# Attention with top-k and a routed mixture of experts on one core: a constant in the fill columns, logits of a batch in two parts, a check of the logits in four parts

## Chip, cores and metric

The kernel runs on one core of a Trainium2 chip. The metric is device time in microseconds (us) of one execution, median of several runs. Engines: PE is TensorE (PEld its weight loads), DVE is VectorE, ACT is ScalarE, POOL is GpSimd, SP is SyncE, which here issues DMAs.

## What is computed

The reference, cut to what matters: attention over 8 batches, 8 heads, 576 positions and 64 features, keeping in each row only scores that reach the 32nd largest, then a mixture of 8 experts in which tokens are assigned greedily by the size of their gate logits.

```
scores = scale * np.matmul(q, k.transpose(0, 1, 3, 2))
kth = np.partition(scores, -top_k, axis=-1)[..., -top_k:-top_k + 1]
scores = np.where(scores >= kth, scores, -1e9)
attn = softmax(scores)
x = (attn @ v).transpose(0, 2, 1, 3).reshape(4608, 512)
logits = x @ w_gate
...
out[mask] = np.maximum(x[mask] @ w1[e], 0.0) @ w2[e]
```

## The kernel before, in words

**Work.** `attention` works through 32 pairs of heads, four pairs (hp 0 to 3) to a batch. A pair has nine tiles of 128 query rows by 576 keys (tile 4 holds the last 64 rows of both heads), so 288 tiles in all. After it `redo` would repeat the attention of pairs that a flag marks (none is marked here; the branch passes over it), and `moe` runs the experts.

**One tile** (`tile_ops`). PE writes the scores into one of three PSUM buffers `s` (`scores`, L218). DVE takes the eight largest of each of six chunks of 96 columns (`chunk`, L221), and from these 48 the first 24 in order (`rank`, L224 to L228). `minus` (L229) makes a bias of the 24th. ACT takes the sign of every score against it and counts with the accumulator (`sign`, L233, into `acc`). By that count, `fill` on DVE (L238) writes eight extra columns 576 to 583 of `s`: a column gets the 24th value, read per row from `st`, where its number in `tab` is under the count, and 0 elsewhere. PE moves the 24 largest out of the way with a matmul (`move` with `off`, L236), DVE takes the next eight over 584 columns (`next8`, L239), of which the last is the cut, PE moves the row back (`move` with `back`), and ACT writes the mask `r` (`relu`, L242) and so sets the buffer `s` free.

**After the tiles** of a pair, `soft` builds transposed scores with the mask in one of two PSUM buffers `pt`, ACT takes the exponential, POOL splits it into two halves of 16 bits, `values` multiplies with v, and ACT scales the result into `xb` (512 rows of the batch) and `xr` (the last 64 rows, the corner).

**Logits** (`logits`, called behind hp 3 only). Five pieces for a batch: four of 128 rows and the corner. For a piece PE transposes the 512 features (L396, four of 128 columns; two in the corner), ACT copies them to `xT` (L398), PE multiplies with the gate weights into another `pt` buffer (L402, L404), and ACT puts the eight logits into `L` (L407, L408).

**Verdict** (`verdict`, L420 to L443). On DVE, behind everything else of attention in its queue: eight instructions on the counts and cuts, three on `L` (is every logit finite, L430 to L432), a matmul on PE that sums over the rows, and a few small ones that write `flags`. All engines read the flag before `moe` starts.

**What sets the order.** `Plan` is a list scheduler: `at` gives every step an engine, a planned duration `d`, and a due time made of the period `PER` and an offset in the table `O`; among the steps that can start within a window `WIN` of the earliest, the one due first goes. The order it finds is the order of each engine's queue; the queues then run in that order and wait on semaphores. SP's queue holds the loads, the transposing DMAs (`turn`, L186, of K and Q; `q2`, L267) and the stores.

Of the kernel before, what the change touches and what calls it, by code (L numbers as in the profile page):

```python
# [99 lines left out]
def attention(tc, q,k,v,w_gate,x_out,L,flags, pairs):  # L100
# [3 lines left out]
    with ExitStack() as ctx:  # L104
# [100 lines left out]
        def tile_ops(P,i):  # L205
# [32 lines left out]
            def fill(): V.tensor_scalar(D["s"][:,576:584],tab,acc[:,col],P["st"][:,i,23:24],op0=ALU.is_lt,op1=ALU.mult)  # L238
# [149 lines left out]
        def logits(P):  # L388
            b=P["b"]; n=P["n"]; t0=(n*9+8)*PER+O["lg"]
            fin=[]  # L390
            for c in range(5):
                p=P["done"]
                D={}; w=512 if c<4 else 256
                def turn(c=c,D=D):
                    D["pt"]=ps_t.tile([128,512],F32,tag="pt",name="ptl")
                    for f in range(4 if c<4 else 2): T.transpose(D["pt"][:,f*128:(f+1)*128],P["x"][0][:,c,f*128:(f+1)*128] if c<4 else P["x"][1][:,2*f:2*f+2,:].rearrange("p a d -> p (a d)"),identf)  # L396
                def copy(D=D,w=w):
                    D["xT"]=wk.tile([128,512],F32,tag="xT",name="xT",bufs=2); A.activation(D["xT"][:,:w],D["pt"][:,:w],AF.Copy)  # L398
                def dot(c=c,D=D):
                    lg=D["lg"]=ps_t.tile([128,512],F32,tag="pt",name="lg"); xT=D["xT"]; o=(b%2)*64  # L400
                    if c<4:
                        for f in range(4): T.matmul(lg[:,:8],xT[:,f*128:(f+1)*128],wg[:,f,:],start=(f==0),stop=(f==3))  # L402
                    else:
                        for i_,(g,a) in enumerate(((0,0),(0,1),(1,0),(1,1))): T.matmul(lg[o:o+64,:8],xT[:,g*128+a*64:g*128+a*64+64],wgr[:,g,a,:],start=(i_==0),stop=(i_==3))  # L404
                def put(c=c,D=D):
                    o=(b%2)*64
                    if c<4: A.activation(L[:,b*4+c,:],D["lg"][:,:8],AF.Copy)  # L407
                    else: A.activation(L[o:o+64,32+b//2,:],D["lg"][o:o+64,:8],AF.Copy)  # L408
                t=t0+O["lgd"]*c
                p=at(t,turn,[p],take="pt",e="P",d=.436); tp=p  # L410
                p=at(t+O["l1"],copy,[p],free=[tp],take="xT",e="A",d=.48); tx=p
                p=at(t+O["l2"],dot,[p],take="pt",free=[tx],e="P",d=.9); tp=p
                p=at(t+O["l3"],put,[p],free=[tp],e="A",d=.07); fin.append(p)
            P["fin"]=at(t0,lambda: None,fin)
            P["done"]=p
        def verdict():

            n9=len(pairs)*9; npr=len(pairs)
            c=cp.tile([128,n9],F32,name="vc"); r=cp.tile([128,n9],F32,name="vr"); ok=cp.tile([128,n9],F32,name="vok")
# [4 lines left out]
            V.scalar_tensor_tensor(ok,c,8.0,ok,op0=ALU.is_le,op1=ALU.mult)
            V.scalar_tensor_tensor(ok,c,0.0,ok,op0=ALU.is_ge,op1=ALU.mult)
            V.scalar_tensor_tensor(ok,cuts,0.0,ok,op0=ALU.is_gt,op1=ALU.mult)
            good=cp.tile([128,npr+1],F32,name="good")
            V.tensor_reduce(good[:,:npr],ok.rearrange("p (n i) -> p n i",i=9),axis=AX.X,op=ALU.add)
            Lf=L.rearrange("p t e -> p (t e)"); fin=cp.tile([128,Lf.shape[1]],F32,name="fin")
# [15 lines left out]
        Ps={}; batch={}
        for n in range(len(pairs)):
# [15 lines left out]
            if P["hp"]==3 or n==len(pairs)-1:  # L462
                logits(P); batch[b]=at((n*9+8)*PER+O["lg"]+O["lgd"]*5,lambda P=P: store(P),[P["fin"]],e="D",d=2.0,late=4.0)
# [485 lines left out]
```

## Time and profile before

| | |
|---|---|
| median of 3 runs | 1474.12 us (1472.0 to 1474.5) |
| profiled execution, its own time | 1470.44 us |
| its span, first to last instruction | 1468.4 us |
| busy over the span | PE 1295.9 us (88%), DVE 1220.3 (83%), ACT 864.6 (59%), POOL 877.2 (60%) |
| attention, first score to last cut | 22.29 to 941.6 us |
| end of attention to the experts' first instruction | 941.6 to 972.03 us |
| experts | 972 to 1468 us |

The profile's page gives a busy share of the whole span, and the stages have different limits; views by stretch and by wait tell which engine ends last in a stage. A busy time counts an instruction up to the end of its write, and the next one on the engine often starts before that: what an instruction takes of its engine's queue is the distance between two starts.

### The profile page before, as it was taken

How to read it: one execution, taken by the hardware profiler on the slowest of the kernel's cores; microseconds unless marked ns; L12 is line 12 of the kernel's file. 1: busy time of each engine (PE TensorE's matmuls, PEld its weight loads, DVE VectorE, ACT ScalarE, POOL GpSimd, SP SyncE). 2: the span in 40 equal slices, each digit the busy share in tenths (PEclk: the TensorE clock that was granted, in tenths of full speed). 3: DMA queues.
4: the chain of work that ended last, by engine and by line, in shares of the span. 5: the costliest groups of instructions: out<-in, count | busy, mean ns of one | idle time of the engine just before them, and what ended most of it. 6: DMA issues, size and time to landing. Idle time of an engine off the chain costs nothing. (4 is left out here: it accounts for less than half of the span.)

```text
span 1468.4 us, 41338 instructions
## 1 busy us (share of the span) xinstructions
PE 1295.9 (88%) x14885; PEld 913.2 (62%) x14886; DVE 1220.3 (83%) x5951; ACT 864.6 (59%) x1922; POOL 877.2 (60%) x1285
## 2 busy tenths in 40 slices
PE   2888998999999999999999899832999999998997
PEld 1666776776776776677677677621655655664663
DVE  4899999999999999999999999658889878887610
ACT  2677777777777777777777787612334424324421
POOL 5688789788788788789879878502043123122211
PEclk9899999999999999999999999955999999999899
DMA  6343363354455445443543452016346346348500
GB/s 130 74 88 78 80 127 84 75 120 91 82 110 97 89 108 84 94 109 77 97 110 83 92 107 46 10 35 170 122 99 198 137 91 198 140 96 271 112 33 33
DMA packets 298149, 149.62 MB, mean 102 GB/s; under 512 B 255440, under 2 KB 280016, under 8 KB 296912
## 3 DMA queue, kind: packets, MB, share of 16 engines
q1 hardware_dynamic: 292048, 128.02, 38.5%
q0 software_dynamic: 5888, 18.88, 4.5%
q8 instruction: 119, 1.95, 0.6%
q14 instruction: 94, 0.77, 0.2%
HBM read 71.34 MB, written 18.87 MB: 61 GB/s over the span
## 5 line engine op out<-in xcount | busy, mean ns | idle before, releaser
L221 DVE MAX8 cd<-s 128x8 f32<-128x96 f32 x1728 | 383.2, 251 | 35.4 <-PE s L218 28.6
L296 POOL TENSOR_TENSOR elm<-F,ehm 128x512 f16<-128x512 f32 x256 | 294.3, 1156 | 6.3
L242 ACT ACTIVATE r<-s,st 128x576 bf16<-128x576 f32 x288 | 213.0, 740 | 98.8 <-PE s L236 93.8
L233 ACT ACTIVATE w<-s,st 128x576 uint16<-128x576 f32 x288 | 213.1, 740 | 95.0 <-DVE st L229 92.9
L895 POOL DMA_INDIRECT out_dram<-ob,idx x40 | 59.0, 1476 | 326.1 <-ACT ob L890 268.2
L239 DVE MAX8 st<-s 128x8 f32<-128x584 f32 x288 | 220.5, 766 | 10.4 <-PE s L236 6.7
L218 PE MATMUL s<-K,Q 128*128 128x512 f16 (+3 forms) x1280 | 195.3, 293 | 28.6 <-DMA Q<-nq 22.3
L856 PE MATMUL ph<-xT,w1h 128*128 128x288 f16 x1024 | 195.8, 289 | 2.0 <-DMA xT<-xs 2.0
L293 POOL TENSOR_SCALAR ehm<-F 128x512 f16<-128x512 f32 x256 | 156.0, 617 | 52.7 <-ACT F L290 52.3
L286 PE MATMUL pt<-Q,K 66*128 66x128 f16 (+1 forms) x1280 | 182.6, 217 | 0.2 <-DMA Q<-nq 0.2
L285 PE MATMUL pt<-Q,K 128*128 128x128 f16 (+1 forms) x1280 | 181.6, 216 | 0.0
L218 PEld LDWEIGHTS <-Q 128*128 128x128 f16 (+1 forms) x1280 | 105.9, 103 | 111.9 <-DMA Q<-nq 22.0
L236 PE MATMUL s<-w,off 128*128 128x512 f16 x576 | 134.1, 290 | 46.8 <-DVE s L238 26.9
L290 ACT ACTIVATE F<-pt 128x512 f32<-128x512 f32 x256 | 150.4, 596 | 20.8 <-PE pt L286 18.5
L856 PE MATMUL ph<-xT,w1l 128*128 128x288 f16 x512 | 147.6, 288 | 0.0
L364 PE MATMUL pv<-vt,E 128*64 128x65 f32 (+1 forms) x1024 | 146.4, 257 | 0.0
L236 PE MATMUL s<-w,back 128*128 128x512 f16 x576 | 120.9, 292 | 23.5 <-DVE st L239 21.7
L865 ACT ACTIVATE hh<-ph 128x288 f16<-128x288 f32 x128 | 52.4, 410 | 146.3 <-PE ph L856 145.4
L285 PEld LDWEIGHTS <-K 128*128 128x128 f16 x1280 | 118.3, 99 | 22.5 <-issue 8.7
L364 PEld LDWEIGHTS <-ehm 128*128 128x128 f16 x2048 | 116.2, 102 | 10.0 <-issue 0.5
L364 PEld LDWEIGHTS pv<-vt,E 128*64 128x64 f32 (+1 forms) x1024 | 113.0, 164 | 14.5 <-issue 3.5
L364 PE MATMUL pv<-vh,ehm 128*128 128x65 f16 x1024 | 120.8, 195 | 0.6 <-ACT F L290 0.6
(252 smaller groups left out, 3271.0 us busy)
## 6 DMA issues: line engine op xcount, KB each, us to landing
wr<-in_moe_w_dram SPq DMA_DIRECT2D x32, 1024.0 KB, 8.2
kn<-in_k_dram SPq DMA_DIRECT2D x64, 128.0 KB, 2.6
qn<-in_q_dram SPq DMA_DIRECT2D x64, 128.0 KB, 2.3
vn<-in_v_dram SPq DMA_DIRECT2D x64, 128.0 KB, 2.3
x<-xb SPq DMA_DIRECT2D x8, 1024.0 KB, 4.8
Q<-nq SPq DMA_TRANSPOSE x160, 3.3
kn<-in_k_dram SPq DMA_DIRECT2D x64, 16.0 KB, 2.3
qn<-in_q_dram SPq DMA_DIRECT2D x64, 16.0 KB, 2.2
```

The costliest lines, as they stand in the source:

```text
L218: T.matmul(s_ps[rows,a:b_],P[Q][:,qc],P[K][:,h*576+a:h*576+b_],start=(Q=="Q1"),stop=(Q=="Q2"))
L221: V.max(D["cd"][:,c*8:c*8+8],D["s"][:,576*c//NCH:576*(c+1)//NCH])
L233: A.activation(D["w"],D["s"][:,:576],AF.Sign,bias=P["st"][:,i,32:33],scale=(1+2.0**-21),accum_out=acc[:,col])
L236: T.matmul(D["s"][:,a:b_],by,w[:,a:b_],start=False,stop=True,skip_group_check=True)
L239: def next8(): V.max(P["st"][:,i,24:32],D["s"][:,:584])
L242: A.activation(r,D["s"][:,:576],AF.Relu,bias=P["st"][:,i,31:32],scale=-1.0)
L285: T.matmul(o,K2[:,kb:kb+128],Q1[:,qc],start=False,stop=False,skip_group_check=True)
L286: T.matmul(o,K3[0:66,kb:kb+128],Q2[0:66,qc],start=False,stop=(c==3 and h==sub[-1][0]),skip_group_check=True)
L293: G.tensor_scalar(D["eh"],D["E"],1.0,0.0,op0=ALU.mult,op1=ALU.add)
L296: G.tensor_tensor(el,D["E"],D["eh"],op=ALU.subtract); P["e"][i]=(D["eh"],el)
L364: for m_ in (range(N-1) if part==0 else (N-1,)): T.matmul(out,seq[m_][0],seq[m_][1],start=(m_==0),stop=(m_==N-1))
L856: P.matmul(B["ph"][:,:288],a[:,c,fs],xT[:,b+c,cs],start=(i==0),stop=(i==11))
```

## The change

It does four things. `fill` takes the constant 2^40 in place of the per-row value. The logits of a batch come in two parts: part 0 behind hp 2, with the first 384 features of the four main pieces and the first half of the corner; part 1 behind hp 3, with the last 128 features of all four pieces in one, and the second half of the corner. The puts into `L` move from ACT to DVE: copies in part 0, additions in part 1. The verdict's look at `L` comes in four parts of it. And the planner's table, period, windows and the planned durations of `fill` and `next8` have new numbers. The experts' code and the order of their instructions are the same. Line numbers behind `fill` grow by 1, behind `verdict` by 13.

```diff
-        PER=4.6166; SP=1.3822; VP=3; WPB=14; EHB=14
-        WIN={'V': 0.027, 'A': 0.079, 'G': 0.008, 'P': 0.138, 'D': 1.472}
+        PER=4.9146; SP=1.9733; VP=3; WPB=14; EHB=14
+        WIN={'V': 0.021, 'A': 0.06, 'G': 0.042, 'P': 0.137, 'D': 1.95}
...
-            def fill(): V.tensor_scalar(D["s"][:,576:584],tab,acc[:,col],P["st"][:,i,23:24],op0=ALU.is_lt,op1=ALU.mult)
+            def fill(): V.tensor_scalar(D["s"][:,576:584],tab,acc[:,col],2.0**40,op0=ALU.is_lt,op1=ALU.mult)
...
-            f_=at(t0+O["j8"],fill,[p],e="V",d=0.075)
+            f_=at(t0+O["j8"],fill,[p],e="V",d=0.12)
...
-            p=at(t0+O["y8"],next8,[p],e="V",d=0.735)
+            p=at(t0+O["y8"],next8,[p],e="V",d=0.685)
...
-        def logits(P):
+        def logits(P,part):
...
+            def piece(k,turns,w,dots,put):
+                D={}; t=t0+O["lgd"]*k
+                def turn():
+                    pt=D["pt"]=ps_t.tile([128,512],F32,tag="pt",name="ptl")
+                    for j,src in enumerate(turns): T.transpose(pt[:,j*128:j*128+128],src(),identf)
...
+                fin.append(at(t+O["l3"],lambda: put(D["lg"]),[p],free=[tp],e="V",d=.08))
...
+            if part==0:
+                for c in range(4):
+                    def dots(lg,xT):
+                        for f in range(3): T.matmul(lg[:,:8],xT[:,f*128:f*128+128],wg[:,f,:],start=(f==0),stop=(f==2))
+                    piece(c,[lambda f=f,c=c: P["x"][0][:,c,f*128:f*128+128] for f in range(3)],384,dots,lambda lg,c=c: V.tensor_copy(L[:,b*4+c,:],lg[:,:8]))
+                piece(4,*corner(0),lambda lg: V.tensor_copy(last,lg[o:o+64,:8]))
+            else:
+                def dots(lg,xT):
+                    for c in range(4): T.matmul(lg[:,c*8:c*8+8],xT[:,c*128:c*128+128],wg[:,3,:],start=True,stop=True)
+                piece(0,[lambda c=c: P["x"][0][:,c,384:512] for c in range(4)],512,dots,lambda lg: V.tensor_tensor(main.rearrange("p c e -> p (c e)"),lg[:,:32],main.rearrange("p c e -> p (c e)"),op=ALU.add))
+                piece(1,*corner(1),lambda lg: V.tensor_tensor(last,lg[o:o+64,:8],last,op=ALU.add))
...
-            V.tensor_tensor(fin,Lf,Lf,op=ALU.subtract)
-            V.tensor_scalar(fin,fin,0.0,None,op0=ALU.is_equal)
-            V.tensor_reduce(good[:,npr:],fin,axis=AX.X,op=ALU.add)
+            for k,(u0,u1) in enumerate(((0,28),(32,35),(28,32),(35,36))):
+                Lf=L[:,u0:u1,:].rearrange("p t e -> p (t e)"); w=8*(u1-u0); fin=cp.tile([128,w],F32,name=f"fin{k}")
+                V.tensor_tensor(fin,Lf,Lf,op=ALU.subtract)
+                V.tensor_scalar(fin,fin,0.0,None,op0=ALU.is_equal)
+                V.tensor_reduce(good[:,npr+k:npr+k+1],fin,axis=AX.X,op=ALU.add); whole.append(128.0*w)
...
-            if P["hp"]==3 or n==len(pairs)-1:
-                logits(P); batch[b]=at((n*9+8)*PER+O["lg"]+O["lgd"]*5,lambda P=P: store(P),[P["fin"]],e="D",d=2.0,late=4.0)
+            if P["hp"]==2: logits(P,0)
+            if P["hp"]==3:
+                P["done"]=at(P["done"]["t"]+.001,lambda: None,[P["done"],Ps[n-1]["fin"]])
+                logits(P,1); P["done"]=P["fin"]; batch[b]=at((n*9+8)*PER+O["lg"]+O["lgd"]*5,lambda P=P: store(P),[P["fin"]],e="D",d=2.0,late=4.0)
```

How the queues change shows at three places.

The queue of SP at the start (nq0 is what the transposes of the first pair's Q read, Q_226 and Q_239 or Q1_234 the two results, kn the second pair's loads of k). Before:

```order
L186 DMA_TRANSPOSE Q2_226<-nq0_159 128x9x128 [waits DMAHW3_49,Pool_49]
L158 DMA kn_231<-in_k_dram 128x256 [waits DMAHW4_49]
L159 DMA kn_231<-in_k_dram 64x64 [waits DMAHW5_49]
L158 DMA kn_231<-in_k_dram 128x256 [waits DMAHW6_49]
L159 DMA kn_231<-in_k_dram 64x64 [waits DMAHW7_49]
L186 DMA_TRANSPOSE Q1_239<-nq0_159 128x9x128 [waits DMAHW0_49,Pool_49]
L158 DMA qn_243<-in_q_dram 128x256 [waits DMAHW1_49]
```

Now:

```order
L186 DMA_TRANSPOSE Q2_226<-nq0_159 128x9x128 [waits DMAHW3_49,Pool_49]
L186 DMA_TRANSPOSE Q1_234<-nq0_159 128x9x128 [waits DMAHW4_49,Pool_49]
L158 DMA kn_236<-in_k_dram 128x256 [waits DMAHW5_49]
L159 DMA kn_236<-in_k_dram 64x64 [waits DMAHW6_49]
L158 DMA kn_236<-in_k_dram 128x256 [waits DMAHW7_49]
L159 DMA kn_236<-in_k_dram 64x64 [waits DMAHW0_49]
L158 DMA qn_264<-in_q_dram 128x256 [waits DMAHW1_49]
```

The second transpose of the first pair's Q now stands ahead of the second pair's four loads of k; before it stood behind them.

The queue of DVE in the fourth pair (tile 33), where the first put of part 0 stands in the changed kernel (lg is a piece's result in PSUM). Before:

```order
L225 MATCH_REPLACE cd2_2513<-st_1138,cd_2456 128x48 [waits DVE_49]
L221 MAX cd_2504<-s_2488 128x8
L226 MAX st_1138<-cd2_2513 128x8 [waits DVE_49]
L221 MAX cd_2504<-s_2488 128x8
L227 MATCH_REPLACE cd2_2513<-st_1138,cd2_2513 128x48 [waits DVE_49]
L221 MAX cd_2504<-s_2488 128x8
L228 MAX st_1138<-cd2_2513 128x8 [waits DVE_49]
```

Now:

```order
L226 MAX st_1138<-cd2_2506 128x8 [waits DVE_49]
L221 MAX cd_2497<-s_2478 128x8
L227 MATCH_REPLACE cd2_2506<-st_1138,cd2_2506 128x48 [waits DVE_49]
L221 MAX cd_2497<-s_2478 128x8
L228 MAX st_1138<-cd2_2506 128x8 [waits DVE_49]
L416 COPY L_61<-lg_2508 128x8 [waits PE_49]
L221 MAX cd_2497<-s_2478 128x8
L229 SCALAR_TENSOR_TENSOR st_1138<-s_2444,st_1138 128x1 [waits DVE_49]
L224 MAX st_1138<-cd_2497 128x8 [waits DVE_49]
L221 MAX cd_2537<-s_2521 128x8 [waits PE_49]
```

Between the ranks and the chunks of two tiles there is now a copy that waits for PE. The rows of the tiles around it keep their pattern; in the whole attention a rank or bias (L224 to L229) follows right behind the instruction whose result it reads 546 times before and 540 times now.

The end of attention in DVE's queue (rs belongs to `values` of the last pair, vc, vr and vok to the verdict on the counts). Before:

```order
L378 RECIPROCAL rs_21710<-rs_21710 128x4 [waits DVE_49]
L344 TENSOR_SCALAR rs_21723<-pv_21705 128x1 [waits PE_49]
L378 RECIPROCAL rs_21723<-rs_21723 128x1 [waits DVE_49]
L420 TENSOR_SCALAR vc_21793<-acc_158 128x288
L421 TENSOR_SCALAR vr_21794<-vc_21793 128x288 [waits DVE_49]
L422 TENSOR_SCALAR vr_21794<-vr_21794 128x288 [waits DVE_49]
L423 TENSOR_TENSOR vok_21795<-vr_21794,vc_21793 128x288 [waits DVE_49]
L424 SCALAR_TENSOR_TENSOR vok_21795<-vc_21793,vok_21795 128x288 [waits DVE_49]
L425 SCALAR_TENSOR_TENSOR vok_21795<-vc_21793,vok_21795 128x288 [waits DVE_49]
L426 SCALAR_TENSOR_TENSOR vok_21795<-cuts_157,vok_21795 128x288 [waits DVE_49,Pool_49]
L428 TENSOR_REDUCE good_21803<-vok_21795 128x32 [waits DVE_49]
L430 TENSOR_TENSOR fin_21805<-L_61 128x288 [waits Activation_49]
```

Now:

```order
L416 COPY L_61<-lg_21818 128x8 [waits PE_49]
L345 TENSOR_SCALAR rs_21844<-pv_21828 128x1 [waits PE_49]
L379 RECIPROCAL rs_21844<-rs_21844 128x1 [waits DVE_49]
L417 COPY L_61<-lg_21841 64x8 [waits PE_49]
L421 TENSOR_TENSOR L_61<-lg_21860,L_61 128x32 [waits PE_49]
L422 TENSOR_TENSOR L_61<-lg_21865,L_61 64x8 [waits DVE_49,PE_49]
L428 TENSOR_SCALAR vc_21873<-acc_158 128x288
L429 TENSOR_SCALAR vr_21874<-vc_21873 128x288 [waits DVE_49]
L430 TENSOR_SCALAR vr_21874<-vr_21874 128x288 [waits DVE_49]
```

The last puts stood in ACT's queue and so beside the verdict's instructions on the counts; now they stand on DVE ahead of these.

## Rows read from the trace of the kernel before

**Rows 1.** Busy us by stretch: length; PE, PEld, DVE, ACT, POOL (count); clock, DMA, GB/s.

```profile
55.40:941.30 885.90, 819.17 (x11127) 619.31 (x11124) 828.91 (x4644) 677.05 (x1587) 735.40 (x1137) 0.99 0.44 90
```

**Rows 2.** Waits of DVE in 56 to 941 us: us in total, times, longest.

```profile
DVE cd L221 <- PE s L218: 10.5, 31, 1.2
DVE st L239 <- PE s L236: 5.7, 15, 1.0
DVE s L238 <- PE s L236: 3.4, 14, 0.3
DVE s L238 <- ACT w L233: 2.1, 14, 0.2
```

**Rows 3.** Timeline of DVE inside attention: start us, duration us, instruction.

```profile
506.53 0.19 DVE L224 MAX8 st<-cd 128x8 f32<-128x48 f32 x1
506.64 0.27 DVE L238 TENSOR_SCALAR s<-tab,acc,st 128x8 f32<-128x8 f32 x1
506.82 0.08 DVE L225 MATCH_VALUE_LOAD cd<-st,cd 128x8 f32 x1
...
507.12 0.21 DVE L226 MAX8 st<-cd 128x8 f32<-128x48 f32 x1
507.36 0.09 DVE L227 MATCH_VALUE_LOAD cd<-st,cd 128x8 f32 x1
```

**Rows 4.** Timeline of DVE in the experts, an instruction with one per-row operand.

```profile
1002.45 0.22 DVE L735 TENSOR_SCALAR w8c<-rev,win 128x8 f32<-128x8 f32 x1
1002.58 0.17 DVE L742 TENSOR_SCALAR pi<-pos 128x36 int32<-128x36 f32 x1
```

**Rows 5.** Timeline of DVE in the experts, a small read of PSUM.

```profile
979.52 0.18 DVE L677 TENSOR_TENSOR cm<-pc,dm 128x32 f32<-128x32 f32 x1
979.63 0.24 DVE L695 TENSOR_SCALAR base<-iTs,lo 128x32 f32<-128x32 f32 x1
```

**Rows 6.** Timeline of SP's queue at the start.

```profile
15.27 1.32 SPq L186 DMA_TRANSPOSE Q<-nq  x1
16.64 0.59 SPq L158 DMA_DIRECT2D kn<-in_k_dram  x1
...
19.00 1.33 SPq L186 DMA_TRANSPOSE Q<-nq  x1
```

**Rows 7.** Timeline of POOL at the start: the last step of the first pair's Q.

```profile
13.30 1.27 POOL L181 TENSOR_TENSOR nq<-sc,nq 128x576 f16<-128x576 f32 x1
```

**Rows 8.** Timeline of PE at the start: its first matmul.

```profile
22.29 3.06 PE L218 MATMUL s<-K,Q 128*128 128x512 f16 x12 [22.29 <-DMA Q<-nq]
```

**Rows 9.** Busy by stretch: a pair with logits, then the three pairs behind it, twice.

```profile
368.20:398.10 29.90, 28.43 (x354) 22.30 (x354) 26.79 (x153) 22.17 (x53) 21.28 (x35) 0.94 0.49 98
398.10:482.50 84.40, 78.59 (x1093) 58.64 (x1090) 80.16 (x450) 65.64 (x154) 74.51 (x114) 1.00 0.49 94
...
597.00:627.90 30.90, 29.45 (x358) 22.43 (x357) 27.44 (x154) 22.20 (x53) 20.36 (x33) 0.93 0.45 93
627.90:713.30 85.40, 78.85 (x1090) 59.14 (x1087) 80.09 (x448) 65.72 (x154) 75.44 (x116) 0.98 0.46 94
```

**Rows 10.** Timeline of ACT at the end of attention.

```profile
954.48 0.32 ACT L346 ACTIVATE xr<-pv,rs 128x64 f32<-128x64 f32 x1 [0.19 <-DVE rs L378]
...
957.68 0.18 ACT L407 ACTIVATE L<-lg 128x8 f32<-128x8 f32 x1 [0.72 <-PE lg L402]
...
963.93 0.17 ACT L408 ACTIVATE L<-lg 64x8 f32<-64x8 f32 x1 [1.11 <-PE lg L404]
```

**Rows 11.** Timeline of DVE at the end of attention.

```profile
954.31 0.29 DVE L420 TENSOR_SCALAR vc<-acc 128x288 f32<-128x288 f32 x1
...
957.36 0.45 DVE L428 TENSOR_REDUCE good<-vok 128x32 f32<-128x288 f32 x1
964.14 0.46 DVE L430 TENSOR_TENSOR fin<-L 128x288 f32<-128x288 f32 x1 [6.33 <-ACT L L408]
...
964.98 0.45 DVE L432 TENSOR_REDUCE good<-fin 128x1 f32<-128x288 f32 x1
```

More of the change, by code (lines that the diff above doesn't have):

```diff
@@ L387, in store @@
                 nc.sync.dma_start(out=x_out[b*576+512:b*576+576,:].rearrange("t (g r d) -> t g r d",r=2,d=64)[:,:,par,:],in_=xr[par*64:par*64+64])
-        def logits(P):
[L389 to L397, printed above, removed]
-                    D["xT"]=wk.tile([128,512],F32,tag="xT",name="xT",bufs=2); A.activation(D["xT"][:,:w],D["pt"][:,:w],AF.Copy)
[L399 to L415, printed above, removed]
@@ new lines, in logits, with copy, dot, corner @@
+        def logits(P,part):
+            b=P["b"]; n=P["n"]; t0=(n*9+8)*PER+O["lg"]; o=(b%2)*64
+            done=P["done"]; fin=[]
+            def piece(k,turns,w,dots,put):
[3 more added lines that the diff above has]
+                    for j,src in enumerate(turns): T.transpose(pt[:,j*128:j*128+128],src(),identf)
+                def copy():
+                    D["xT"]=wk.tile([128,512],F32,tag="xT",name="xT",bufs=2); A.activation(D["xT"][:,:w],D["pt"][:,:w],AF.Copy)
+                def dot():
+                    D["lg"]=ps_t.tile([128,512],F32,tag="pt",name="lg"); dots(D["lg"],D["xT"])
+                p=tp=at(t,turn,[done],take="pt",e="P",d=.11*len(turns))
+                p=tx=at(t+O["l1"],copy,[p],free=[tp],take="xT",e="A",d=.06+w*.00083)
+                p=tp=at(t+O["l2"],dot,[p],take="pt",free=[tx],e="P",d=.224*len(turns))
+                fin.append(at(t+O["l3"],lambda: put(D["lg"]),[p],free=[tp],e="V",d=.08))
+            main=L[:,b*4:b*4+4,:]; last=L[o:o+64,32+b//2,:]
+            def corner(g):
+                def dots(lg,xT):
+                    for a in range(2): T.matmul(lg[o:o+64,:8],xT[:,a*64:a*64+64],wgr[:,g,a,:],start=(a==0),stop=(a==1))
+                return [lambda: P["x"][1][:,2*g:2*g+2,:].rearrange("p a d -> p (a d)")],128,dots
+            if part==0:
[5 more added lines that the diff above has]
+            else:
+                def dots(lg,xT):
+                    for c in range(4): T.matmul(lg[:,c*8:c*8+8],xT[:,c*128:c*128+128],wg[:,3,:],start=True,stop=True)
+                piece(0,[lambda c=c: P["x"][0][:,c,384:512] for c in range(4)],512,dots,lambda lg: V.tensor_tensor(main.rearrange("p c e -> p (c e)"),lg[:,:32],main.rearrange("p c e -> p (c e)"),op=ALU.add))
+                piece(1,*corner(1),lambda lg: V.tensor_tensor(last,lg[o:o+64,:8],last,op=ALU.add))
+            P["fin"]=at(t0,lambda: None,fin); P["lgdone"]=fin[-1]
@@ L426, in verdict @@
             V.scalar_tensor_tensor(ok,cuts,0.0,ok,op0=ALU.is_gt,op1=ALU.mult)
-            good=cp.tile([128,npr+1],F32,name="good")
+            good=cp.tile([128,npr+4],F32,name="good")
             V.tensor_reduce(good[:,:npr],ok.rearrange("p (n i) -> p n i",i=9),axis=AX.X,op=ALU.add)
-            Lf=L.rearrange("p t e -> p (t e)"); fin=cp.tile([128,Lf.shape[1]],F32,name="fin")
-            V.tensor_tensor(fin,Lf,Lf,op=ALU.subtract)
-            V.tensor_scalar(fin,fin,0.0,None,op0=ALU.is_equal)
@@ L432, in verdict @@
-            V.tensor_reduce(good[:,npr:],fin,axis=AX.X,op=ALU.add)
+            whole=[]
+            for k,(u0,u1) in enumerate(((0,28),(32,35),(28,32),(35,36))):
[3 more added lines that the diff above has]
+                V.tensor_reduce(good[:,npr+k:npr+k+1],fin,axis=AX.X,op=ALU.add); whole.append(128.0*w)
@@ L433, in verdict @@
             ones=cp.tile([128,1],F32,name="ones1"); V.memset(ones,1.0)
+            want=cp.tile([1,npr+4],F32,name="want"); V.memset(want[:,:npr],1152.0)
+            for k,x_ in enumerate(whole): V.memset(want[:,npr+k:npr+k+1],x_)
             pt=ps_t.tile([128,512],F32,tag="pt",name="ptv")
-            T.matmul(pt[:1,:npr+1],ones,good,start=True,stop=True)
-            bad=cp.tile([1,npr+1],F32,name="bad"); V.tensor_copy(bad,pt[:1,:npr+1])
-            V.tensor_scalar(bad[:,:npr],bad[:,:npr],-1.0,1152.0,op0=ALU.mult,op1=ALU.add)
@@ L438, in verdict @@
-            V.tensor_scalar(bad[:,npr:],bad[:,npr:],-1.0,128.0*Lf.shape[1],op0=ALU.mult,op1=ALU.add)
-            V.tensor_scalar(bad[:,:npr],bad[:,:npr],bad[:,npr:],None,op0=ALU.add)
+            T.matmul(pt[:1,:npr+4],ones,good,start=True,stop=True)
+            bad=cp.tile([1,npr+4],F32,name="bad"); V.tensor_tensor(bad,want,pt[:1,:npr+4],op=ALU.subtract)
+            nf=cp.tile([1,1],F32,name="nf"); V.tensor_reduce(nf,bad[:,npr:],axis=AX.X,op=ALU.add)
+            V.tensor_scalar(bad[:,:npr],bad[:,:npr],nf,None,op0=ALU.add)
@@ L440, in verdict @@
             fl=cp.tile([1,npr],F32,name="flf"); V.tensor_scalar(fl,bad[:,:npr],0.0,None,op0=ALU.not_equal)
+            V.tensor_reduce(nf,fl,axis=AX.X,op=ALU.add)
+            V.tensor_copy(flags[:,npr:npr+1],nf)
             V.tensor_copy(flags[:,0:npr],fl)
-            V.tensor_reduce(bad[:,npr:],fl,axis=AX.X,op=ALU.add)
-            V.tensor_copy(flags[:,npr:npr+1],bad[:,npr:])
         Ps={}; batch={}
```

2 lines of the change are left out of this document (1 added, 1 removed).

## Prediction, made before the changed kernel ran

> **What bounds the kernel now.** I looked first at the steady part of attention, in the view of busy time by stretch: from 55.4 to 941.3 us DVE is busy for 828.9 of 885.9 us, 94% [rows 1]. PE shows nearly as much, 819.2 us, but its matmuls are pipelined and their ends modelled, so that figure overstates it; POOL stands at 735.4 and ACT at 677.1. Which of DVE and PE waits for the other is read from the view of waits: in this whole stretch DVE waits for PE and ACT for only 10.5 + 5.7 + 3.4 + 2.1 = 21.7 us [rows 2]. So DVE is the engine with hardly any slack, and the other 35 us that it isn't busy are its own gaps. The timeline of DVE shows one: a MAX8 whose successor needs nothing of it is followed after 506.64 - 506.53 = 0.11 us, one whose successor reads its result after 507.36 - 507.12 = 0.24 us [rows 3]. From this I take that a shorter DVE instruction in attention shortens the time by about as much, and a longer or added one lengthens it. PE, ACT and POOL set the time only where DVE would have to wait for them. Two places lie outside this rule: the start, where PE waits for a DMA until 22.29 us [rows 8], and the end of attention, where the last cut is done near 941 us and a serial chain through ACT, PE and DVE follows [rows 10, 11]. The experts behind it keep their code and order, so I give them no term.
>
> **Fill: 288 instructions with one per-row operand less.** The fill starts at 506.64 and the next instruction at 506.82, so it takes 0.18 us of the queue with two per-row operands, the count and the 24th value [rows 3]. With one per-row operand and the same 128 x 8 size, the instruction in the experts takes 1002.58 - 1002.45 = 0.13 us [rows 4]. That one writes SBUF, the fill writes PSUM, so the row is near but not the same. I take the difference, 0.05 us: 288 x 0.05 = 14.4 us less. Bounds: nothing, if the write to PSUM and not the operand makes the fill long; and 0.07 us (20.2 us), if the one-operand fill gets as short as a 0.11 us MAX8 of 48 columns in the same rows. All of it lies on DVE, so I count all of it. The new planned durations of fill and next8 change no duration on the chip.
>
> **Puts: 56 instructions more on DVE.** A batch has five copies and two additions in place of five puts on ACT: 7 x 8 = 56, of which 48 are 8 columns wide and 8 are 32 wide. They read PSUM. The nearest row is a 128 x 32 addition-like instruction from PSUM in the experts: it lasts 0.18 us, and the next starts 979.63 - 979.52 = 0.11 us behind it [rows 5]. 56 x 0.11 = 6.2 us more; the lower bound is half of it, if copies of eight columns are shorter. Each put also waits for PE, and everything behind it in DVE's in-order queue waits with it: ranks, biases and fills of the tiles in work, and through them ACT's sign and PE's moves. Today a wait of the same kind, next8 for a move, costs 5.7 us over 279 tiles, 0.02 us each [rows 2]; 56 x 0.02 = 1.1 us more. What ACT loses, 40 puts, is hidden: ACT has 209 us free in the stretch [rows 1].
>
> For such an instruction the Trainium skill speaks against the change: VectorE: DVE Perf Modes, section "The TRN2 errata", gives VectorE 120 cycles at 0.96 GHz plus one for each column from PSUM to SBUF. By that, as an estimate from that page, the puts would take 48 x 133 + 8 x 158 ns = 7.7 us, and the sum below would be smaller by 1.5 us. The trace doesn't agree with taking this as time of the queue: the row of 32 columns [rows 5] is followed after 0.11 us, not 0.158.
>
> **Logits in two parts: the same matmuls, other places.** PE has 16 transposes and 16 small matmuls of the main rows and 2 + 4 of the corner for a batch, before and now. ACT's copies change in width only and lie beside DVE's work. What can change is the bunching. Before, four of the five pieces come at once in the pair behind a batch; now they are spread over nearly a whole pair. Two pairs with logits took 29.9 and 30.9 us, where a third of the three pairs behind them is 84.4 / 3 = 28.1 and 85.4 / 3 = 28.5 us [rows 9]: 1.8 and 2.4 us lost, and in just these two the granted clock of PE is 0.94 and 0.93 against 1.00 and 0.98 behind them, a mean over 2.4 GHz with some us at 1.2 GHz. Whether the clock falls there again I can't see from the order. I take 1.0 us less, between 3 us more (two further dips of that price or so) and 4.2 us less (both gone).
>
> **Start.** On SP's queue the second transpose of the first pair's Q now stands ahead of four loads. It was issued at 19.00 and the one ahead of the loads at 15.27, done issuing at 16.59; the first load starts at 16.64 [rows 6]. The data that it reads were ready at 13.30 + 1.27 = 14.57 [rows 7]. So it goes out at 16.64, 2.36 us earlier, and PE's first matmul, which waited for it [rows 8], comes 2.4 us earlier, with everything behind it. The four loads get later by one transpose, 1.3 us; their pair is needed only a pair later, 28 us on. If that were wrong, at most these 2.4 us come back.
>
> **End.** Before, the last scaling in ACT ends at 954.80, the second piece's put at 957.86, the last at 964.10 [rows 10]: three rounds in 9.3 us. Now only two pieces are left behind the last scaling, one round of 957.86 - 954.80 = 3.1 us. But a remaining piece of part 0 and its copy on DVE stand ahead of the last matmuls of the values; I let them cost 0.8 us (bounds 0 and 1.5, half a round). The logits end near 958.7 and not 964.1. Against that, the verdict on the counts, 954.31 to 957.81, ran beside the logits [rows 11] and now stands behind the last addition: 3.5 us in series. The look at L took 964.14 to 965.43 = 1.3 us and becomes twelve instructions: some 1.1 us for the wide three and 3 x 0.24 us for each of three small sets, each instruction waiting for the one ahead [rows 3], 3.3 us. 958.7 + 3.5 + 3.3 = 965.5 against 965.4: no gain, give or take 1.5 us. What is late next is DVE itself.
>
> **The rest of the new order.** The table moves instructions in every pair. I can't price that row by row. Counted in the order, a rank or bias stands right behind its own input 546 times before and 540 times now; at 0.13 us each that is under 1 us. I take nothing, and keep 4 us either way.
>
> **Sum.** -14.4 + 6.2 + 1.1 - 1.0 - 2.4 + 0 = -10.5 us. The profiled execution took 1470.4 us, so 1459.9 on its scale; the median of the runs shown is 3.7 us above it, so 1474.1 - 10.5 = **1463.6 us**.
>
> **Rivals.**
> 1. *The puts block DVE (slower).* A put that stands ahead of its matmuls holds the queue that bounds the kernel. It decides by the mean wait of a put: from 0.21 us on (56 x 0.21 - 1.1 = 10.7) the gain is gone, and from 0.26 us on (13.5 us more) the kernel is slower by over 0.2%, 2.9 us, about what a measurement can tell from no change. At 0.4 us, a third of the longest wait of DVE for PE [rows 2], it is 22.4 - 1.1 = 21.3 us more: 1484.9. For it: nothing but the order keeps the matmuls ahead. Against it: the waits for PE in the same queue are short today. Chance 0.11.
> 2. *The saving turns into waits (the same time).* Each tile holds one of three score buffers, and DVE's work on three tiles hides the round through PE and ACT. If that round, not DVE, is the limit, the 14.4 us only lengthen waits: 1463.6 + 14.4 = 1478.0 with none of it kept, 1473 with a third. For it: PE at 92% busy. Against it: 21.7 us of waits in 886 [rows 2] says the round is mostly hidden. Chance 0.13.
> 3. *More than that.* The fill falls by 0.07 us (5.8 us more), the copies take half (3.1 us), and the clock stays up in the pairs with logits (3.2 us): 1451.5. Chance 0.13.
>
> The forecast keeps 0.63. Its own range, with the fill between 0.03 and 0.07 us and 4 us for the order, is 1457 to 1470.
>
> **How the numbers follow.** Faster by over 0.2%: the forecast and rival 3, and a little of rival 2: 0.78. Within 0.2%: most of rival 2, 0.09. Slower: rival 1 and the end of rival 2: 0.13. The range 1452 to 1475 leaves out rival 1, half of rival 3 and the end of rival 2, under 0.2.
>
> **What would show it.** The fill's duration falls from 0.27 us to about 0.22, and it is followed after 0.13 us. DVE's waits for the pieces' matmuls stay near 1 us in all; over 15 us would mean rival 1. Waits of DVE for PE s rising by 10 us would mean rival 2. PE's first matmul starts near 19.9 us. The last cut lies near 931 us, and between it and the experts' first instruction there are still some 30 us. If the fill is as long as before, the main term is wrong; if attention's steady part isn't 6 to 10 us shorter, the reading that DVE bounds it is.

## Result and profile after

| | before | changed |
|---|---|---|
| median of the runs shown (us) | 1474.31 (1472.0 to 1478.34) | 1458.0 (1451.83 to 1458.23) |
| ratio, 95% interval | | 0.9876 [0.9843, 0.991] |
| profiled execution / its span (us) | 1470.44 / 1468.4 | 1458.23 / 1456.5 |
| start to the last cut of pair 0 | 55.7 | 52.6 |
| steady part: from there to the last cut | 885.9 | 878.8 |
| last cut to DVE's first step of the experts | 29.2 | 28.5 |
| experts | 497.5 | 496.7 |

The change made the kernel 16.3 us faster by the medians, 12.2 us between the two profiled executions (that of before lay 3.9 us under its median, the changed one's 0.2 us above). Of the 11.9 us between the spans, 7.1 came out of the steady part, 3.1 out of the start, 0.7 out of the end, and 0.8 out of the experts, whose code is the same (they took 492.3 to 499.0 us over the runs below). DVE's first step of the experts is a wait for a semaphore, which the timelines leave out; by the memset behind it, at 972.03 us before and at 960.43 now, the end takes 30.4 and 29.0 us and the experts 496.3 and 496.1.

The steady part of the changed kernel, in the view of busy time by stretch (columns as in [rows 1]):

```profile
52.60:931.40 878.80, 815.42 (x11154) 616.04 (x11152) 818.71 (x4693) 677.38 (x1570) 732.75 (x1133) 1.00 0.45 91
```

DVE has 10.2 us less to do than in [rows 1], with 49 rows more. Its waits in the same stretch (us in total, times, longest):

```profile
DVE cd L221 <- PE s L218: 15.4, 40, 1.3
DVE s L239 <- ACT w L233: 6.7, 26, 0.4
DVE st L240 <- PE s L236: 1.3, 5, 0.6
DVE s L239 <- PE s L236: 1.2, 3, 0.8
DVE L L416 <- PE lg L415: 0.8, 1, 0.8
DVE rs L345 <- PE pv L365: 0.8, 4, 0.2
```

They add up to 26.2 us against 21.7 before [rows 2], 4.5 us more. The copies (L416) waited once, for 0.8 us. DVE's timeline shows a fill (L239), its neighbours and a copy (start us, duration us, instruction):

```profile
492.87 0.19 DVE L224 MAX8 st<-cd 128x8 f32<-128x48 f32 x1
492.98 0.21 DVE L239 TENSOR_SCALAR s<-tab,acc 128x8 f32<-128x8 f32 x1
493.10 0.09 DVE L225 MATCH_VALUE_LOAD cd<-st,cd 128x8 f32 x1
...
494.57 0.16 DVE L416 COPY L<-lg 128x8 f32<-128x8 f32 x1
494.65 0.20 DVE L228 MAX8 st<-cd 128x8 f32<-128x48 f32 x1
```

Between the same two neighbours as in [rows 3] the fill is followed after 0.12 us, before after 0.18; over all 288 fills the mean is 0.139 us, before 0.197. The copy is followed after 0.08 us here. At the start, SP's queue and PE's first matmul, which answer to [rows 6, 8]:

```profile
15.62 2.73 SPq L186 DMA_TRANSPOSE Q<-nq  x2
18.39 0.58 SPq L158 DMA_DIRECT2D kn<-in_k_dram  x1
```

```profile
20.42 3.06 PE L218 MATMUL s<-K,Q 128*128 128x512 f16 x12 [20.42 <-DMA Q<-nq]
```

Both transposes go out ahead of the loads, and PE starts 1.87 us earlier. The end of attention on ACT and then on DVE, which answers to [rows 10, 11]:

```profile
944.03 0.32 ACT L347 ACTIVATE xr<-pv,rs 128x64 f32<-128x64 f32 x1 [1.14 <-DVE rs L379]
```

```profile
931.92 0.17 DVE L416 COPY L<-lg 128x8 f32<-128x8 f32 x1 [0.54 <-PE lg L415]
939.01 0.16 DVE L345 TENSOR_SCALAR rs<-pv 128x4 f32<-128x4 f32 x1 [6.92 <-PE pv L365]
...
946.68 0.19 DVE L421 TENSOR_TENSOR L<-lg,L 128x32 f32<-128x32 f32 x1 [2.55 <-PE lg L420]
947.01 0.17 DVE L422 TENSOR_TENSOR L<-lg,L 64x8 f32<-64x8 f32 x1
947.19 0.31 DVE L428 TENSOR_SCALAR vc<-acc 128x288 f32<-128x288 f32 x1
...
947.88 0.31 DVE L430 TENSOR_SCALAR vr<-vr 128x288 f32<-128x288 f32 x1
...
950.27 0.45 DVE L436 TENSOR_REDUCE good<-vok 128x32 f32<-128x288 f32 x1
950.64 0.38 DVE L440 TENSOR_TENSOR fin<-L 128x224 f32<-128x224 f32 x1
...
953.12 0.16 DVE L442 TENSOR_REDUCE good<-fin 128x1 f32<-128x8 f32 x1
...
954.89 0.16 DVE L454 CAST flags<-flf 1x32 int32<-1x32 f32 x1
```

From the end of the last scaling (944.35) to the end of the second addition (947.18) it is 2.8 us, one round, where three rounds took 9.3. Behind it the verdict on the counts (L428 to L436, 3.5 us) and the four looks (2.6 us) follow in series on DVE, which had nothing to do from 932.1 to 939.0 us. The last flag is written at 955.05, 23.7 us behind the last cut. Before it was 25.7 us:

```profile
967.13 0.14 DVE L443 CAST flags<-bad 1x1 int32<-1x1 f32 x1
```

These 2.0 us repeat in a second pair of profiles (below). The table shows only 0.7 of them, because the time from the last flag to the experts differs from execution to execution: 3.6 and 4.7 us in two of the kernel before, 4.8 and 5.1 us in two of the changed one.

### The profile page after: what moved, and what is told of

Same layout as the page of the kernel before. It is cut to its first block, busy times and chain, and to the rows that moved or that the text cites. A ratio compares the mean times of both kernels' runs of the same rounds, so it can differ in the third digit from the quotient of the medians.

```text
span 1456.5 us, 41407 instructions
## 1 busy us (share of the span) xinstructions
PE 1284.9 (88%) x14885; PEld 903.7 (62%) x14886; DVE 1211.4 (83%) x6020; ACT 863.1 (59%) x1898; POOL 875.8 (60%) x1285
## 5 line engine op out<-in xcount | busy, mean ns | idle before, releaser
L221 DVE MAX8 cd<-s 128x8 f32<-128x96 f32 x1728 | 373.4, 252 | 35.4 <-PE s L218 30.8
L287 PE MATMUL pt<-Q,K 66*128 66x128 f16 (+1 forms) x1280 | 179.2, 216 | 0.0
L286 PE MATMUL pt<-Q,K 128*128 128x128 f16 (+1 forms) x1280 | 178.3, 215 | 0.0
L218 PEld LDWEIGHTS <-Q 128*128 128x128 f16 (+1 forms) x1280 | 104.9, 103 | 108.8 <-DMA Q<-nq 20.1
L291 ACT ACTIVATE F<-pt 128x512 f32<-128x512 f32 x256 | 150.7, 597 | 15.4 <-PE pt L287 10.4
L365 PE MATMUL pv<-vl,ehm 128*128 128x65 f16 x1024 | 120.8, 192 | 0.0
```

The source lines that it names most:

```text
L218: T.matmul(s_ps[rows,a:b_],P[Q][:,qc],P[K][:,h*576+a:h*576+b_],start=(Q=="Q1"),stop=(Q=="Q2"))
L221: V.max(D["cd"][:,c*8:c*8+8],D["s"][:,576*c//NCH:576*(c+1)//NCH])
L286: T.matmul(o,K2[:,kb:kb+128],Q1[:,qc],start=False,stop=False,skip_group_check=True)
L287: T.matmul(o,K3[0:66,kb:kb+128],Q2[0:66,qc],start=False,stop=(c==3 and h==sub[-1][0]),skip_group_check=True)
L365: for m_ in (range(N-1) if part==0 else (N-1,)): T.matmul(out,seq[m_][0],seq[m_][1],start=(m_==0),stop=(m_==N-1))
```

## Experiments

Lengths are read as in the table above, in the profiled execution of each run. The time between the last cuts of two pairs repeats from run to run, in most pairs within 0.03 us, except where the granted clock fell in it. So the sharpest measure of the steady part, which holds 7.75 batches, is an undisturbed batch: for each of the four places in a batch the mean of the pairs without such a fall, added up. Each ratio is to the kernel before in the same series; its medians there were 1471.3 to 1474.3 us, so a few us between medians of two series can be the series.

**Parts of the change.** The first kernel is the kernel before with the constant alone; all queues keep their order.

```diff
-            def fill(): V.tensor_scalar(D["s"][:,576:584],tab,acc[:,col],P["st"][:,i,23:24],op0=ALU.is_lt,op1=ALU.mult)
+            def fill(): V.tensor_scalar(D["s"][:,576:584],tab,acc[:,col],2.0**40,op0=ALU.is_lt,op1=ALU.mult)
```

> The kernel before with the constant in the fill and nothing else; every queue keeps its order. Theory 1 (DVE bounds attention, so what the fill loses the kernel loses): the profile of the changed kernel shows the next instruction 0.12 us behind the fill in place of 0.18, so 288 x 0.06 = 17 us less, about 1457 us where before takes 1474. Theory 2 (the gain is the new order and the spread logits; the fill's saving turns into waits of DVE): within 4 us of before, and DVE's waits for PE and ACT in attention rise from 22 to some 35 us.

Measured: 1457.09 us, ratio 0.9904 [0.9877, 0.9932]. The steady part:

```profile
56.24:927.89 871.65, 814.06 (x11121) 617.58 (x11120) 812.82 (x4643) 675.03 (x1587) 735.30 (x1137) 0.99 0.45 92
```

It is 14.3 us shorter than before, and the batch fell from 113.54 to 111.76 us: 1.78 / 36 = 0.049 us for each fill. DVE's waits rose from 21.7 to 24.7 us, not to 35. The second kernel is the changed one with the per-row value put back (the reverse of the same line).

> The changed kernel with the per-row value back in the fill; every queue keeps its order. Theory 1: 17 us more than the changed kernel, about 1475 us, that is, level with before. Theory 2: 1458 to 1462 us, the gain stays.

Measured: 1469.9 us, ratio 0.9983 [0.9969, 0.9997].

```profile
53.22:943.66 890.44, 817.19 (x11154) 615.74 (x11152) 834.04 (x4694) 678.24 (x1570) 731.17 (x1133) 1.00 0.44 90
```

The steady part is 11.6 us longer than the changed kernel's, the batch 114.86 against 112.98: 1.88 / 36 = 0.052 us for each fill; DVE's waits are 23.2 us against 26.2. So in both orders 0.05 us of the 0.06 that the queue shows reaches the time, and the waits take the rest. The rest of the change, without the constant, is worth 0.2%, while the constant alone brings most of the whole: a ratio of 0.9904 against 0.9876, with intervals that overlap.

**Code and table crossed.** The third kernel is the changed code with the old table (period, windows and all offsets), the fourth the old code with the new table.

```diff
-        PER=4.9146; SP=1.9733; VP=3; WPB=14; EHB=14
-        WIN={'V': 0.021, 'A': 0.06, 'G': 0.042, 'P': 0.137, 'D': 1.95}
+        PER=4.6166; SP=1.3822; VP=3; WPB=14; EHB=14
+        WIN={'V': 0.027, 'A': 0.079, 'G': 0.008, 'P': 0.138, 'D': 1.472}
```

> The changed kernel's code with the planner's table, period and windows of before (the planned durations stay new). Theory 1: the table is worth little, 1455 to 1466 us. Theory 2: the table carries the gain, 1468 us or more.

> The kernel before with the planner's table, period and windows of the change. Theory 1: within 6 us of before. Theory 2: 1458 to 1464 us. A third possibility, that a table suits only the code it was made with, would show as several us slower here and in the run with the new code and the old table alike.

Measured: 1479.19 us, ratio 1.0059 [1.0038, 1.0079], and 1484.61 us, ratio 1.0082 [1.0056, 1.0109]. Both are slower than before. DVE's waits in the fourth:

```profile
DVE cd L221 <- PE s L218: 13.1, 34, 1.6
DVE st L239 <- PE s L236: 11.0, 24, 0.5
DVE s L238 <- ACT w L233: 7.5, 18, 1.1
DVE s L238 <- PE s L236: 7.4, 25, 0.4
DVE cd L221 <- PE s L236: 3.0, 3, 1.0
```

They come to 42.0 us, in the third to 46.1 us, some 20 more than with the table that belongs to the code. Each of the two tables does worse with the other's code, the third possibility, so neither cross shows what the logits in two parts are worth by themselves. The start does follow the table: PE's first matmul comes at 22.7 us with the old one and at 20.1 with the new one, whatever the code.

**The price of a put.** The fifth kernel moves the 40 copies of part 0 to ACT.

```diff
-... lambda lg,c=c: V.tensor_copy(L[:,b*4+c,:],lg[:,:8]))
+... lambda lg,c=c: A.activation(L[:,b*4+c,:],lg[:,:8],AF.Copy))
```

> The changed kernel with the 40 copies of the first part of the logits (32 of the main pieces, 8 of the small corner) on ScalarE in place of VectorE; TensorE's order is the same. Theory 1 (VectorE sets the length of the steady part, and a copy costs it the 0.06 us by which the next instruction starts behind it): the steady part falls by 40 x 0.06 = 2.4 us, from 878.8 to about 876.4, the median from 1458.0 to about 1455.6. Rival 1 (the copies hold VectorE up, at 0.21 us each or more with their waits): the steady part falls by 8.4 us or more, to 870.4 or less. Rival 2 (what VectorE is spared turns into waits, or ScalarE is late with its evictions instead): the steady part is 878 or longer, and VectorE's waits grow by what was saved.

Measured: 1449.46 us, ratio 0.9836 [0.9811, 0.986], steady part 871.9 us. The pair with the most copies, in the changed kernel and then in this one (busy time by stretch):

```profile
365.57:393.61 28.04, 26.25 (x349) 20.11 (x347) 25.80 (x150) 21.70 (x51) 20.54 (x34) 1.00 0.37 79
```

```profile
363.46:391.00 27.54, 25.79 (x346) 19.94 (x345) 25.61 (x147) 21.84 (x54) 20.49 (x34) 1.00 0.38 81
```

The batch fell from 112.98 to 112.34 us: 0.64 / 5 = 0.13 us for each copy, twice what was expected. Over all 50 puts ahead of 928 us the next instruction starts 0.06 to 0.20 us behind, 0.114 in the mean. That comes near to 0.13, but by chance, as a comparison of the two traces shows. Their queues hold the same order, so the distance between a copy's two neighbours can be read with the copy and without it. For 14 of the 35 copies ahead of 915 us nothing changed. They stand in a chain, such as between a chunk (L221) and the rank that reads it, which start 0.35 us apart with the copy and without it:

```profile
364.21 0.26 DVE L221 MAX8 cd<-s 128x8 f32<-128x96 f32 x1
364.38 0.15 DVE L416 COPY L<-lg 128x8 f32<-128x8 f32 x1
364.56 0.21 DVE L224 MAX8 st<-cd 128x8 f32<-128x48 f32 x1
```

```profile
362.10 0.25 DVE L221 MAX8 cd<-s 128x8 f32<-128x96 f32 x1
362.45 0.21 DVE L224 MAX8 st<-cd 128x8 f32<-128x48 f32 x1
```

For 18 copies between instructions that don't need each other it is 0.06 to 0.08 us less without them, and for three copies of the corner 0.32 us less. These three are in every second batch, in rows 64 to 127 and not 0 to 63, and start only when the instruction ahead has ended, as the next one does behind them (0.20 us). All 35 make 2.2 us, 0.31 a batch.

The larger part is one wait, which repeats in each of the seven batches. Behind the second copy DVE stood 0.49 us for the scores of a tile, and now stands 0.07. In PE's queue the transposes of the next piece (L398) are ahead of these scores. In the changed kernel they were released when ACT's exponential `E` ended:

```profile
364.51 0.60 ACT L291 ACTIVATE E<-pt 128x512 f32<-128x512 f32 x1
365.16 0.55 PE L398 MATMUL ptl<-identf,xb 128*128 128x128 f32 x3 [0.40 <-ACT E L291]
366.23 0.27 DVE L221 MAX8 cd<-s 128x8 f32<-128x96 f32 x1 [0.50 <-PE s L218]
```

In the fifth kernel the copy on ACT, which stands ahead of `E`, released them:

```profile
362.40 0.17 ACT L416 ACTIVATE L<-lg 128x8 f32<-128x8 f32 x1
362.63 0.55 PE L398 MATMUL ptl<-identf,xb 128*128 128x128 f32 x3
363.70 0.27 DVE L221 MAX8 cd<-s 128x8 f32<-128x96 f32 x1
```

So 0.42 us a batch come from a release on PE and 0.31 from DVE's queue, and some 0.08 go back into another wait for scores. The exponentials, the pieces and their results share the two `pt` buffers; that this decides the release is a guess, which no run here shows.

The sixth kernel issues each copy of the four main pieces five times.

```diff
-... lambda lg,c=c: V.tensor_copy(L[:,b*4+c,:],lg[:,:8]))
+... lambda lg,c=c: (V.tensor_copy(L[:,b*4+c,:],lg[:,:8]),[V.tensor_copy(spare[:,j,:],lg[:,:8]) for j in range(4)]))
```

> The changed kernel with each of the 32 copies of a main piece's first part issued five times, the four further ones into a tile that nothing reads: 128 added copies of 128x8. Theory 1 with the spacing that the changed kernel's trace shows (the next instruction starts 0.06 us behind a copy): the steady part grows by 128 x 0.06 = 7.7 us, from 878.8 to 886.5, the median from 1458.0 to about 1465.7. At the price that the prediction took for a put (0.11 us): 14.1 us, to 892.9 and 1472.1. Rival 2 (VectorE has slack): under 2 us. Rival 1 (copies from PSUM block VectorE and so TensorE): 0.21 us each and more, 27 us or more.

Measured: 1459.15 us, ratio 0.9903 [0.988, 0.9926], steady part 879.7 us. Four copies in a row on DVE:

```profile
137.17 0.37 DVE L416 COPY spare<-lg 128x8 f32<-128x8 f32 x4
137.46 0.20 DVE L224 MAX8 st<-cd 128x8 f32<-128x48 f32 x1
```

They start 0.073 us apart, 0.29 us for four. Between a copy's two neighbours they add 0.17 us in a chain and up to 0.29 elsewhere, 0.25 in the mean or 1.0 us a batch. But the batch grew from 112.98 to 113.56 us only: 0.58 / 16 = 0.036 each. Neither the expected 7.7 us nor the 14.1 came. Of the 1.0 us some 0.4 disappear, most of it in DVE's idle time, which is 0.3 us a batch shorter than in the seventh kernel, whose steady part is the changed kernel's. So DVE does not bound every moment, and a price for a spread instruction doesn't hold for a lump, nor the other way round.

**The end.** The seventh kernel splits the verdict in `counts`, `look` and the rest, and moves the counts and two of the looks (parts 0 to 28 and 32 to 35) behind the last pair's clear.

```diff
+        P=Ps[len(pairs)-1]; p=at(P["clear"]["t"],counts,[P["clear"]],e="V",d=3.5)
+        p=at(P["clear"]["t"]+.01,lambda: (look(0,0,28),look(1,32,35)),[p,Ps[27]["fin"]],e="V",d=1.6)
```

> The changed kernel with the check of the counts (eight VectorE instructions, 3.7 us from L428 to the end of L436) and the look at the parts 0 to 28 and 32 to 35 of the logits placed right behind the last pair's clear, where VectorE waits from 932.1 to 939.0 us; only the looks at the two last parts stay behind the last addition. Theory 1 (behind the last addition VectorE alone sets the time up to the flags): the stretch from the last cut to the experts falls from 28.5 us to about 23.3, the steady part stays at 878.8, and the median falls from 1458.0 to about 1453. Rival (the experts wait for something else there, the transposed x on ScalarE for one, or the added work makes the divisors of the last pair late): the stretch falls by less than 1.5 us, and the median stays within 1456.5 to 1459.5.

Measured: 1452.12 us, ratio 0.9854 [0.9829, 0.9879]. The end shrank from 28.5 to 25.0 us, 3.5 and not 5.2. Its DVE timeline (its lines 427 to 435 are the changed kernel's 428 to 436), and GpSimd's:

```profile
930.08 1.21 DVE L429 TENSOR_SCALAR vr<-vr 128x288 f32<-128x288 f32 x1
...
937.95 0.18 DVE L442 TENSOR_REDUCE good<-fin 128x1 f32<-128x24 f32 x1
938.05 0.16 DVE L345 TENSOR_SCALAR rs<-pv 128x4 f32<-128x4 f32 x1
```

```profile
929.97 1.16 POOL L297 TENSOR_TENSOR elm<-F,ehm 128x512 f16<-128x512 f32 x1
```

L429 (L430 of the changed kernel) took 1.21 us instead of 0.31; it started beside GpSimd's pass `elm` and ended 0.16 us behind it. So the moved work took 9.0 us (929.11 to 938.13), the divisors `rs` of the last pair stood behind it, and by the last cut they came 9.6 us behind (928.49 to 938.05), before 7.6. The Trainium skill, GPSIMD Engine Reference, section "Key points", has the two engines contend for their SBUF interfaces where the VectorE instruction runs in a two-port mode or has two SBUF inputs. The trace agrees for L433, which has two inputs and took 1.23 us beside two passes of `elm` and 0.46 without (L434 of the changed kernel); L429 has one, and whether it runs in a two-port mode no run shows. The eighth kernel joins this edit and the copies on ACT.

> The two edits together: first-part copies on ScalarE, counts and early looks behind the last pair's clear. Theory 1: both gains add, 2.4 + 5.2 us: steady part about 876.4, last cut to experts about 23.3, median about 1450.4, which would beat both kernels. Rival 2: no gain from the copies and under 1.5 us from the end, 1456 or more.

Measured: 1447.5 us, ratio 0.9823 [0.9797, 0.9848]; steady part 871.5, end 24.7 us: by these parts the gains add. By the medians only 2.0 us of the end's 3.7 show against the fifth kernel; the six executions spread from 1443.7 to 1452.2 us. In the ninth the two looks wait for the last pair's last transposes (kept as `P["turn"]`), so that only the counts stand beside GpSimd's passes.

```diff
-        p=at(P["clear"]["t"]+.01,lambda: (look(0,0,28),look(1,32,35)),[p,Ps[27]["fin"]],e="V",d=1.6)
+        p=at(P["turn"]["t"]+.01,lambda: (look(0,0,28),look(1,32,35)),[p,Ps[27]["fin"],P["turn"]],e="V",d=1.6)
```

> The two edits of the run before (first-part copies on ScalarE, counts early), with the two early looks moved from behind the counts to the stretch behind the last pair's divisors, where VectorE waited 2.55 us for the last dots and GpSimd has nothing left. Theory (GpSimd's elm passes hold VectorE's counts up: L429 took 1.21 us beside one and 0.31 without, and this made the divisors 1.9 us late): the counts now end before the divisors are due, so the stretch from the last cut to the experts falls from 24.7 to about 23.4, the median from 1447.5 to about 1446.2. Rival (the late divisors cost nothing, or the looks now make the last addition late): the stretch stays at 24.5 or more.

Measured: 1443.44 us, ratio 0.9799 [0.9784, 0.9814], the fastest of all. Its end is 23.4 us, as expected:

```profile
929.84 0.45 DVE L435 TENSOR_REDUCE good<-vok 128x32 f32<-128x288 f32 x1
...
931.22 0.16 DVE L345 TENSOR_SCALAR rs<-pv 128x4 f32<-128x4 f32 x1 [0.89 <-PE pv L365]
...
936.12 0.37 DVE L440 TENSOR_TENSOR fin<-L 128x224 f32<-128x224 f32 x1
...
938.83 0.19 DVE L421 TENSOR_TENSOR L<-lg,L 128x32 f32<-128x32 f32 x1 [1.07 <-PE lg L420]
```

The divisors wait for PE again and not for DVE, and the looks lie in a wait that still has 1.07 us left. The two kernels share the steady part (870.9 and 871.5), so 1.3 us of the 4.1 between their medians come from the end. The rest is not explained; the two were measured in different series.

**TensorE's clock.** The changed kernel and the kernel before once more, for the stretches in which the granted clock is 0.5.

> The changed kernel once more, for TensorE's clock. If the stretches at the granted clock of 0.5 come from where the logits stand: none or one of 3.4 us in the steady part, and the pairs with the first part of the logits at 28.0 to 28.5 us each without one. If they come by chance: as many as in the kernel before, three to five.

> The kernel before once more, for the same question: three to five stretches of 3.4 us at 0.5 in the steady part, each making its pair 1.2 to 2 us longer than the 28.6 of a pair that carries the logits and has none. If by chance: none or one is as likely.

Measured: 1457.93 and 1473.59 us. In the steady part the kernel before had six such stretches of 3.4 us (in the first profile five), all but one in a pair with logits or at its edge, the constant alone four; the changed kernel had two both times (one of the first profile is 6.8 us long and begins 2 us ahead of the steady part), and the other kernels with its order none or one (six profiles). Neither count was in its expected band, but the direction is the expected one in every profile. Why the clock falls there is not shown. A pair with part 0 in the changed kernel that had one, and the same pair of the seventh kernel, without one:

```profile
704.16:734.03 29.87, 27.99 (x349) 21.23 (x347) 26.13 (x151) 21.86 (x51) 21.44 (x34) 0.94 0.39 80
```

```profile
702.56:730.87 28.31, 26.44 (x349) 20.23 (x347) 26.02 (x150) 21.69 (x51) 20.56 (x34) 1.00 0.39 79
```

A stretch at 1.2 GHz costs its pair 1.56 us here. What the steady part has over 7.75 undisturbed batches of its own profile was 5.9 and 7.7 us in the kernel before, 3.2 and 2.2 us in the changed one; this holds the falls and what the first and the last pairs have of their own. The second pair of spans differs by 15.4 us: 10.1 in the steady part, 2.3 at the start, 1.6 at the end and 1.5 in the experts.

## Why the prediction was right

The forecast was 1463.6 us, faster; measured was 1458.0. On the scale of the profiled executions it was 10.5 us less and 12.2 came. By its steps, with the steady part taken apart by undisturbed batches (113.54 before, 111.76 with the constant, 112.98 changed, each times 7.75) and what lies over them:

| step | predicted (us) | measured (us) |
|---|---|---|
| fill | -14.4 | -13.8 in the steady part (-14.6 in the new order) |
| puts, their waits, rest of the order | +6.2 + 1.1 + 0 | +9.5 together |
| logits' bunching and the clock | -1.0 | -2.8 (-5.5 in the second pair of profiles) |
| start | -2.4 | -3.1 |
| end | 0 | -0.7 (-2.0 up to the last flag) |
| experts | none | -0.8 |
| sum | -10.5 | -11.7; the spans differ by 11.9 |

- *DVE bounds the steady part*: right for what is spread over all tiles. The constant took 0.05 us from each of 288 fills, alone and inside the change. The term hit its size by two errors that cancel: the fill left the queue 0.06 us sooner, not 0.05 as the step from [rows 3] to [rows 4] said, and a sixth of that went into waits. The sixth kernel shows the limit of the sentence: of the time by which 128 added copies move their neighbours apart, some 40% cost nothing.
- *Puts at 0.11 us and 0.02 us of waits*: the total was right, by luck in its parts. 40 copies taken away gave back 0.13 us each. But a copy's own share is 0.06 us in the mean, as the expectations of the fifth and sixth kernel had it, and nothing where it stands in a chain. The other half is mainly the wait of 0.42 us a batch, and that one comes from a release on PE, not from a put that waits for its matmul. The Trainium skill (VectorE: DVE Perf Modes, "The TRN2 errata") gives, by an estimate from that page, 0.133 us for a copy of eight columns from PSUM; the trace, with 0.06 to 0.20 us between starts, doesn't agree with it as a fixed time in the queue.
- *The rest of the order at nothing*: undersized. Of the 9.5 us, the fifth kernel gives 5.0 to the 40 copies with what hangs on them; 4.5 us are left for the 16 additions and the order. At the predicted 0.13 us each the additions would be 2.1 of them, an estimate, so the order stays inside the 4 us that were kept. No run separates them further.
- *Logits and clock*: the right sign, a third to a fifth of the size. The two falls that [rows 9] showed were two of five.
- *Start*: right in kind, 1.87 us and not 2.4 at PE's first matmul; the rest of the 3.1 fell inside pair 0, where the fill is shorter too; it wasn't taken apart.
- *End at nothing*: nearly right. As was said, the gain of one round against three was mostly eaten by the counts in series, but the last flag came 2.0 us sooner, where 1.5 were allowed. That this could be had back was not seen: 5.1 us by the ninth kernel.
- *Rival 1* (puts block DVE): shown wrong by 0.8 us of waits for their matmuls, and by 0.13 us for a copy with all that hangs on it, where 0.21 was its threshold. *Rival 2* (all turns into waits): shown wrong by 26.2 us of waits against 21.7. *Rival 3*: the fill's slot and the clock went its way, the copies didn't.

The net: the constant is the gain. The puts and the new order cost 9.5 us, about what the clock, the start and the end bring (2.8 + 3.1 + 0.7), with 3 us left over as cost. That is the sum over one pair of profiles; by the ratios, 0.9876 for the whole against 0.9904 for the constant alone, the rest brings a little. Whether it costs or brings some us stays open.

## What to carry to other kernels

Price an instruction on the bounding engine by how far it moves its two neighbours apart, not by its duration and not by the distance to the next instruction: here that was 0.06 to 0.08 us between independent neighbours and nothing in a chain. A sixth (the fills) to two fifths (the lumps of copies) of it vanished in that engine's waits. Then ask what the instruction's end releases on other engines: two thirds of what the copies gave back on ACT was a wait for PE. When work moves to the bounding engine while another has room, try it on the other: the copies on ACT gave 5.0 us in undisturbed batches (7.75 x 0.64), and 0.4% by the ratios (0.9876 and 0.9836). Serial work at the end of a stage can move into an earlier wait of its engine, but look at which neighbours run there: beside GpSimd the same instruction took up to four times as long.

## What was not expected of the hardware

- A VectorE instruction of 128 x 288 with one input took 0.31 us alone and 1.21 us beside a two-input GpSimd pass of 1.16 us.
- A 128 x 8 copy from PSUM lasts 0.15 us and is followed after 0.06 to 0.20 us; taken away, it brings its neighbours 0.06 to 0.08 us closer where they don't need each other, and not at all inside a chain.
- Corner copies and additions in rows 64 to 127 of their tiles (every second batch) are followed after 0.20 us, those in rows 0 to 63 after 0.06 us.
- A fill with one per-row operand in place of two is followed 0.06 us sooner.
- Some falls of the granted clock to 0.5 repeat by place: at 730 and 729 us in two profiles of the changed kernel, at 622 and 620, 710 and 709 in two of the kernel before.
